# Attention and MoE on one core: inverse row sums by way of DRAM, their product on GpSimd, swapped queries by DMA, other buffer counts

## The chip, the cores and the metric

The kernel runs on one core of one Trainium2 chip. The metric is the device time of one execution in microseconds (us). A core has the engines TensorE (PE; its weight loads are shown apart as PEld), VectorE (DVE), ScalarE (ACT), GpSimd (POOL) and SyncE (SP), which issues nearly all DMAs here. Each engine runs its own instructions in order; semaphores order the engines among each other.

## The reference

Attention in which a query sees only the keys of its own hash bucket, then a gated MoE-like product over all tokens.

```python
# q, k, v: (4, 8, 768, 64), proj: (64, 6)
q_bits = np.einsum('bhsd,dk->bhsk', q, proj) > 0
k_bits = np.einsum('bhsd,dk->bhsk', k, proj) > 0
mask = q_bucket[:, :, :, None] == k_bucket[:, :, None, :]   # buckets: the 6 bits as a number
scores = np.where(mask, (1 / np.sqrt(D)) * q @ k.T, -1e9)
attn = np.exp(scores - scores.max(-1, keepdims=True))
attn = attn / (attn.sum(-1, keepdims=True) + 1e-9)
x = (attn @ v).transpose(0, 2, 1, 3).reshape(3072, 512)
gate = 1 / (1 + np.exp(-(x @ w_gate)))                      # w_gate, w_val: (512, 1536)
out = (gate * (x @ w_val)) @ w_out                          # w_out: (1536, 512)
```

## The kernel before

**Pairs and groups.** The 32 heads (4 batches of 8) are worked off in 16 pairs of heads (`pair`, L601). Each pair has 6 tiles of 128 queries, in two groups of three tiles (`group`, L696), so there are 32 groups.

**Preparing a pair.** `load` fetches k and q. The queries' tile `qr` has three columns of 64 for each row: head 0, head 1, head 0 again, so that `turn` (L626) can transpose both the pair (head 0, head 1), named q, and the swapped pair (head 1, head 0), named qs, from it. A turn is 12 small transposes on PE into a double PSUM bank (tag "two", three of them). `high` (L641) copies the result to SBUF in a rounded form (ACT or DVE), and `low` (L645, DVE) makes the rest, so that a product of high and low parts has nearly float32 precision. This gives kh/kl, qh/ql and qsh/qsl, two buffers of each. `hash_` multiplies with the projection on PE and `bits_q`, `bits_k` make +-masks on DVE (qb, kb). The pair's scores start only after all of `needs`: the low parts and the bits.

**Scores.** `scores(t, h)` is 8 matmuls (three products of high and low parts, and one of the bits, each in two row halves of the array), for 768 keys into a "two" bank. The swapped queries put head 1's queries into the rows of head 0's keys and the reverse, so both halves of the array work. `maximum` (L718, DVE) takes the row maximum and moves the scores to SBUF (tile `e`), `exponent` (L739, ACT) makes the exponentials in place and their row sums into a column of `su`.

**The rest of a group.** After its six exponentials: `guard` and `inverse` (DVE) turn the row sums into inverse sums, 6 columns of 128 rows. The product with v comes out transposed (head columns on partitions, queries along the row), so the inverse sums are needed along the row, the same on 64 partitions: `spread` (L754) does it by 6 matmuls of the broadcast column with the identity into a bank (tag "one"; each is two instructions, 12 in all), and `spread_copy` moves it to SBUF (`rb`). `turned(c)` (L768) transposes the probabilities of one chunk of 128 keys (12 transposes), `whole` copies them to SBUF (`ef`), and `values(c)` (L790) multiplies with v, four instructions a chunk, accumulated over six chunks in a "one" bank (`pv`). `summed` multiplies pv by rb on DVE into `xs`, and `store` sends it to the DRAM tensor xd.

**The MoE.** `moe_early` does a third of the hidden columns (J1 = 3 blocks of 128) of the first three batches, between the attention of later pairs; its units are spread over the scores' progress. `load_w` turns the weights from 64-bit floats into high and low parts on DVE, ACT and POOL, and keeps most of them in DRAM. After all stores of the attention, `switch` gives the attention's memory free, the kept weights are fetched, and `moe_late` does the rest. `load_x` and `gated` split x and the gated product into parts on ACT, POOL and DVE.

**Order.** Nothing of this is ordered by hand. Every step is added to a `Plan` (L58) with a key (its due place; t0 is 6 for each pair and 3 for each group), an engine or a choice of engines, an estimate of its ns, the steps it comes after, and the buffers that it takes and gives. `order` (L74) simulates the engines with these estimates and writes the steps in the order in which they start, so the estimates decide each engine's program order. `stock` counts the buffers. PE steps name the array's tiling: "rows" (two row halves: scores, transposes), "columns" (two column halves: spread, values) or all; the plan counts a change of it with 95 ns. 60 filler matmuls (`busy`, L270) stand at the lowest key.

Of the kernel before, what the change touches and what calls it, by code (L numbers as in the profile page):

```python
# [9 lines left out]
F32 = mybir.dt.float32  # L10
F32R = mybir.dt.float32r
# [8 lines left out]
P = 128  # L20
# [3 lines left out]
EPS = 1e-9  # L24
# [33 lines left out]
class Plan:  # L58
# [115 lines left out]
def lsh_attention_glu_kernel(ctx, tc, q, k, v, proj, w_gate, w_val, w_out, out):  # L174
    nc = tc.nc
    B, H, S, D = q.shape
# [3 lines left out]
    NC = S // P  # L180
    GT = 3
    NG = NC // GT
    GN = GT * P
    HP = H // 2
# [6 lines left out]
    f = lambda ap: ap.bitcast(F32)  # L191
# [4 lines left out]
    const = ctx.enter_context(tc.tile_pool(name="const", bufs=1))  # L196
    dram = ctx.enter_context(tc.tile_pool(name="dram", bufs=1, space=bass.MemoryType.DRAM))
    xd = [dram.tile([HP, P, S], F32, name=f"xd{b}") for b in range(B)]
    part = [dram.tile([NG, GT, P, DM], F32, name=f"part{b}") for b in range(B)]

    kept = {(n, j): dram.tile([P, 2, DM], F32, name=f"k{n}{j}") for n in "gvo" for j in range(J1, NJ)}
# [2 lines left out]
    ps = ctx.enter_context(tc.tile_pool(name="ps", bufs=2, space=PSUM))  # L204
    ident = const.tile([P, P], F32, name="ident")
# [37 lines left out]
    for n, signs, groups in (("q", (1.0, -1.0), ALL), ("k0", (-1.0, 1.0), ALL[::2]), ("k1", (-1.0, 1.0), ALL[1::2])):  # L243
        w = const.tile([P, P], F32, name=f"hw{n}", tag="hw")
        nc.vector.memset(w, 0.0)
        for g in groups:
            half = g % 2 if n == "q" else g // 2
            rows = slice(half * D, (half + 1) * D)
            for i, sign in enumerate(signs):
                at_ = g * HB + i * NB  # L250
                nc.vector.tensor_scalar_mul(w[rows, at_ : at_ + NB], praw[rows], sign)
        hi, lo = hw[n] = [const.tile([P, P], F32R, name=f"hw{n}{x}") for x in "hl"]
        nc.scalar.copy(hi, w)
        nc.vector.tensor_sub(lo, w, f(hi))
    mp = ctx.enter_context(tc.tile_pool(name="moe", bufs=1))
    xp = ctx.enter_context(tc.tile_pool(name="xp", bufs=1))
    w1 = ctx.enter_context(tc.tile_pool(name="w1", bufs=1))
# [2 lines left out]
    at = ph1.enter_context(tc.tile_pool(name="attn", bufs=2))  # L260
# [9 lines left out]
    def busy():  # L270
# [1 line left out]

    W_KEY, W_STEP = 12.0, 2.2
    stock = dict(
        one=1, two=3, moe=1, z=2, y=4, kr=2, qr=2, vr=2, h=2, e=10, st=3, su=3, rb=1, xs=2,
        ef=6, raw1=1, mid1=1, wk=1, xr=1, x=1, ob=3,
    )
    plan = Plan(stock)
    add = plan.add

    MM, MO, TH = 174, 231, 62
    FF = 644
# [3 lines left out]
    def dma(key, nbytes, emit, **kw):  # L286
        return add(key, "sp", 600, emit, tail=2000 + nbytes // 200, **kw)
# [300 lines left out]
    sp = lambda t: t.rearrange("p (j n) -> p j n", j=2)  # L588
# [3 lines left out]
    halves = [slice(0, D), slice(D, P)]  # L592


    def either(copied, n=1):
        return [
            ("act", 60 + 315 * n, lambda: copied(nc.scalar.copy)),
            ("dve", 70 + 400 * n, lambda: copied(nc.vector.tensor_copy)),
        ]

    def pair(i):  # L601
        b, hp = heads[i]
        u = f"{b}_{hp}"
        t0 = i * NC
        z = {}
        two = slice(2 * hp, 2 * hp + 2)

        def load(n):

            if n == "k":  # L610
                z[n] = at.tile([P, 2, GT, 2, D], F32, name=f"kr{u}", tag="kr", bufs=stock["kr"])
                from_ = k[b, two].rearrange("h (p c) d -> p h c d", c=NC)
                for h in range(2):
                    for j in range(2):
                        nc.sync.dma_start(z[n][:, h, :, j], from_[:, h, j * GT : (j + 1) * GT])
            else:
                z[n] = at.tile([P, NC, 3, D], F32, name=f"qr{u}", tag="qr", bufs=stock["qr"])
                from_ = q[b, two].rearrange("h (p c) d -> p h c d", c=NC)
                for m in range(3):
                    nc.sync.dma_start(z[n][:, :, m], from_[:, m % 2])  # L620

        def load_v():
            z["v"] = at.tile([P, 2, NC, D], F32, name=f"vr{u}", tag="vr", bufs=stock["vr"])
# [2 lines left out]
        def turn(n):  # L626

            z["t", n] = pt = ps2.tile([P, 2, 512], F32, name=f"t{n}{u}", tag="two")
            flat = z[n[0]].rearrange("p a b c d -> p (a b c d)" if n == "k" else "p a b d -> p (a b d)")
            step, first = (P, 0) if n == "k" else (3 * D, (n == "qs") * D)  # L630
            for m in range(NC):
                for r, rows in enumerate(halves):
                    nc.tensor.transpose(
                        pt[:, r, m * D : (m + 1) * D], flat[rows, m * step + first : m * step + first + P],
                        ident[rows, rows], tile_position=(r * D, 0),
                    )

# [6 lines left out]

        def low(n):  # L645
            nc.vector.tensor_sub(ordered(z[n + "l"]), turned_(n), f(ordered(z[n + "h"])))  # L646

        def hashed(acc, w, n, j):
            for m, (a, x) in enumerate(((1, "h"), (0, "l"), (0, "h"))):
# [21 lines left out]
            n: add(t0 - 10.72, "sp", 2400, lambda n=n: load(n), tail=4000, take=[n + "r"]) for n in "kq"  # L671
        }
        needs, last_turn = [], None
        for m, n in enumerate(("k", "q", "qs")):
            n_ = t0 - 6 + m
            last_turn = add(
                n_, "pe", 2 * NC * TH // 2 + 50, lambda n=n: turn(n), after=[here[n[0]], last_turn],
                take=["two"] + ["h"] * (m == 0), give=[n + "r"] if n == "k" else ["qr"] * (n == "qs"), tiles="rows",
            )
            a = add(n_, either(lambda copy, n=n: high(n, copy), 2), after=[last_turn])  # L680
            needs.append(add(n_, "dve", 880, lambda n=n: low(n), after=[a], give=["two"]))
        for m, n in enumerate("kq"):
            n_ = t0 - 2.8 + m * 0.6
            a = add(n_, "pe", 6 * MM, lambda n=n: hash_(n), after=[needs[m]], take=["two"])
            if n == "k":
                needs += [
                    add(n_, "dve", 590, lambda h=h: bits_k(h), after=[a], give=["two"] * h) for h in range(2)
                ]
            else:
                needs.append(add(n_, "dve", 990, bits_q, after=[a], give=["two"]))  # L690
        v_here = dma(t0 - 5, 393216, load_v, take=["vr"])

        for g in range(NG):
# [2 lines left out]
    def group(i, g, z, needs, v_here):  # L696
        b, hp = heads[i]
        u = f"{b}_{hp}_{g}"
        t0 = i * NC + g * GT
        gz = {}  # L700
# [36 lines left out]
            )  # L737

        def exponent(t, h):  # L739
            if t == 0 and h == 0:  # L740
                gz["su"] = at.tile([P, 2, GT], F32, name=f"su{u}", tag="su", bufs=stock["su"])
            e, st = gz["e", t, h], gz["st", t]
            nc.scalar.activation(  # L743
                e, e, AF.Exp, bias=st[:, 2, h : h + 1], scale=st[:, 1, h : h + 1],
                accum_out=gz["su"][:, h, t : t + 1],
            )

        def guard():
            nc.vector.tensor_scalar_add(gz["su"], gz["su"], EPS)

        def inverse():
            nc.vector.reciprocal(gz["su"], gz["su"])

        def spread():  # L754

            gz["rs"] = rs = ps.tile([P, 512], F32, name=f"rs{u}", tag="one")
            for t in range(GT):
                for h, rows in enumerate(halves):
                    nc.tensor.matmul(  # L759
                        rs[rows, t * P : (t + 1) * P], gz["su"][:, h, t : t + 1].broadcast_to([P, D]), ident,  # L760
                        start=True, stop=True, tile_position=(0, h * D),
                    )

        def spread_copy(copy):
            gz["rb"] = at.tile([P, GN], F32, name=f"rb{u}", tag="rb", bufs=stock["rb"])
            copy(gz["rb"], gz["rs"][:, :GN])

        def turned(c):  # L768

# [27 lines left out]
                    start=(c == 0), stop=(c == NC - 1), tile_position=(0, h * D),  # L797
                )

        def summed():  # L800
            gz["xs"] = at.tile([P, GN], F32, name=f"xs{u}", tag="xs", bufs=stock["xs"])
            nc.vector.tensor_mul(gz["xs"], gz["pv"][:, :GN], gz["rb"])

        def store():
            nc.sync.dma_start(xd[b][hp][:, g * GN : (g + 1) * GN], gz["xs"])
# [18 lines left out]
                    take=["su"] if t == 0 and h == 0 else [], give=["st"] * (h == 1),  # L824
                ))
        n = t0 - 0.78
        a = add(n, "dve", 90, guard, after=exps)
        inverse_ = add(n, "dve", 90, inverse, after=[a])
        chunks, last = {}, None
        for c in range(NC):  # L830
            n = t0 + LAG + c * 0.4
# [1 line left out]
                       give=["e"] * GT * 2 if c == NC - 1 else [], tiles="rows", kind="turn")  # L833
            chunks[c] = add(n, either(lambda copy, c=c: whole(c, copy), 2), after=[last], give=["two"])
        n = t0 + LAG + 3
        a = add(n, "pe", FF, spread, after=[inverse_], take=["one"], give=["su"], tiles="columns")
        spread_ = add(n, either(spread_copy), after=[a], take=["rb"], give=["one"])
        prev = None
        for c in range(NC):
            prev = add(  # L840
# [75 lines left out]
```

## Time and profile before

| | us |
|---|---|
| median of 3 runs (1119.0 to 1120.32) | 1119.46 |
| the profiled execution, own time | 1119.6 |
| its span, first to last instruction | 1117.8 |
| PE busy | 1095.1 |
| DVE busy | 564.8 |
| ACT busy | 505.1 |
| POOL busy | 231.6 |

In the profile, times are in us unless marked ns; L12 is line 12 of the kernel. A row of the groups by line gives line, engine, operation, output<-inputs, shapes and count, then total busy time and mean ns of one, then the engine's idle time just before them and what ended it. A row of the timeline gives start, length, engine, line and what was done, with neighbours of one kind merged. A row of the waits gives who waited for whom, the total, the number and the longest. PE's matmuls are pipelined, so lengths overlap: what a matmul costs in a row of others is the distance between starts. "q" behind an engine's name is its sequencer, which issues DMAs.

### The profile page before, as it was taken

To read this page: it belongs to the slowest core of one execution; us is meant where nothing else is said; L and a number is where in the kernel's file an instruction comes from. 1 tells how busy PE (TensorE), PEld (TensorE's weight loads), DVE (VectorE), ACT (ScalarE), POOL (GpSimd) and SP (SyncE) were. 2 spreads that over 40 slices of the span, in tenths; PEclk is the share of its full clock that TensorE was granted. 3 is DMA by queue.
4 is the path that set the end of the run, shared out by engine and by line. 5 is a ranking of instruction groups with operands and counts; after the bars stand their busy time and mean duration, and the time that the engine had idled before them with its cause. 6 is when DMAs were issued, how large, how long until landed. Compare 5 with 4: busy or idle time off the path is not lost.

```text
span 1117.8 us, 21374 instructions
## 1 busy us (share of the span) xinstructions
PE 1095.1 (98%) x8980; PEld 874.8 (78%) x8988; DVE 564.8 (51%) x1204; ACT 505.1 (45%) x898; POOL 231.6 (21%) x210
## 2 busy tenths in 40 slices
PE   9999999999999999999999999999999999999998
PEld 5666676677667677676667899999999999999997
DVE  7888878888879788887774101001020202020201
ACT  4766676667667676676665212212121212121211
POOL 0101224122324213312001112112121212121211
PEclk9999999999999999999999999999999999999999
DMA  8323343544544435531101860002020201010010
GB/s 189 89 61 97 106 135 99 157 148 151 169 139 140 140 120 162 179 126 54 49 15 46 320 242 28 31 1 85 1 85 1 69 17 59 26 51 34 7 51 28
DMA packets 110655, 103.61 MB, mean 93 GB/s; under 512 B 66784, under 2 KB 94432, under 8 KB 110560
## 3 DMA queue, kind: packets, MB, share of 16 engines
q1 hardware_dynamic: 110400, 102.26, 29.1%
q8 instruction: 70, 1.15, 0.4%
q14 instruction: 25, 0.20, 0.1%
q10 hardware_dynamic: 160, 0.00, 0.0%
HBM read 70.78 MB, written 31.46 MB: 91 GB/s over the span
## 4 chain that ended last, share of the span: by engine, by line
PE 84%; DVE 9%; POOL 2%; ACT 2%; issue 1%; POOLq 0%; DVEq 0%
PE pv L795 12%; PE sc L709 8%; PE zv_0l L424 7%; PE zv_1l L424 7%; PE zg_0l L424 7%; PE zg_1l L424 7%; PE yo_0l L457 7%; PE yo_1l L457 6%; PE tp L778 6%; DVE e L723 4%; PE zo L457 4%; PE zg L424 3%; PE zv L424 2%; PE sc L714 2%; PE rs L759 2%
## 5 line engine op out<-in xcount | busy, mean ns | idle before, releaser
L743 ACT ACTIVATE e<-e,st 128x768 f32<-128x768 f32 x192 | 196.7, 1026 | 77.6 <-DVE st L735 73.5
L723 DVE TENSOR_SCALAR_CACHE_REDUCE e<-sc 128x768 f32<-128x768 f32 x192 | 177.2, 951 | 32.7 <-PE sc L714 32.4
L795 PE MATMUL pv<-ef,vr 128*64 128x384 f32 x768 | 136.9, 494 | 0.3 <-issue 0.3
L440 DVE TENSOR_TENSOR gf_0l<-zv_0l,sig 128x384 f32<-128x384 f32 x39 | 21.7, 557 | 210.2 <-PE zv_0l L424 210.2
L440 DVE TENSOR_TENSOR gf_1l<-zv_1l,sig 128x384 f32<-128x384 f32 x39 | 21.8, 558 | 208.9 <-PE zv_1l L424 208.9
L778 PEld LDWEIGHTS tp<-ident,e 64*128 64x128 f32 x2304 | 81.7, 138 | 34.7 <-issue 18.3
L785 DVE COPY ef<-tp 128x768 f32<-128x768 f32 x99 | 91.6, 951 | 33.2 <-PE tp L778 32.8
L778 PE MATMUL tp<-ident,e 64*128 64x64 f32 x2304 | 95.9, 227 | 8.9 <-DVE ql L646 2.4
L795 PEld LDWEIGHTS pv<-ef,vr 128*64 128x64 f32 x768 | 49.8, 136 | 56.8 <-issue 44.6
L709 PE MATMUL sc<-kh,qsl 64*128 64x384 f32 x192 | 85.7, 447 | 2.2 <-DVE e L723 1.9
L424 PE MATMUL zg_0l<-xh_0l,wg 128*128 128x384 f32 x312 | 86.4, 337 | 0.0
L424 PE MATMUL zg_1l<-xh_1l,wg 128*128 128x384 f32 x312 | 86.4, 337 | 0.0
L709 PE MATMUL sc<-kh,ql 64*128 64x384 f32 x192 | 85.7, 447 | 0.3 <-issue 0.3
L424 PE MATMUL zv_1l<-xh_1l,wv 128*128 128x384 f32 x312 | 85.5, 334 | 0.0
L424 PE MATMUL zv_0l<-xh_0l,wv 128*128 128x384 f32 x312 | 85.5, 334 | 0.0
L785 ACT COPY ef<-tp 128x768 f32<-128x768 f32 x93 | 73.2, 796 | 25.5 <-PE tp L778 24.9
L445 POOL TENSOR_TENSOR gl<-gf_0l,gh 128x384 fp32r<-128x384 f32 x39 | 40.8, 1047 | 185.4 <-ACT gh L444 185.4
L445 POOL TENSOR_TENSOR gl<-gf_1l,gh 128x384 fp32r<-128x384 f32 x39 | 40.4, 1037 | 184.5 <-ACT gh L444 184.5
L457 PE MATMUL yo_0l<-wo,gh 128*128 128x512 f32 x234 | 73.5, 395 | 0.0
L457 PE MATMUL yo_1l<-wo,gh 128*128 128x512 f32 x234 | 73.5, 395 | 0.0
L576 ACT ACTIVATE sig<-zg_1l 128x384 f32<-128x384 f32 x39 | 19.2, 492 | 116.1 <-PE zg_1l L424 116.1
L576 ACT ACTIVATE sig<-zg_0l 128x384 f32<-128x384 f32 x39 | 19.2, 492 | 111.0 <-PE zg_0l L424 111.0
(165 smaller groups left out, 2572.2 us busy)
## 6 DMA issues: line engine op xcount, KB each, us to landing
qr<-in_q_dram SPq DMA_DIRECT2D x48, 192.0 KB, 4.0
kr<-in_k_dram SPq DMA_DIRECT2D x64, 96.0 KB, 2.6
vr<-in_v_dram SPq DMA_DIRECT2D x16, 384.0 KB, 3.7
rawg<-in_moe_w_gate_dram SPq DMA_DIRECT2D x12, 512.0 KB, 4.0
xd<-xs SPq DMA_DIRECT2D x32, 192.0 KB, 2.9
rawv<-in_moe_w_val_dram SPq DMA_DIRECT2D x12, 512.0 KB, 3.7
rawo<-in_moe_w_out_dram SPq DMA_DIRECT2D x12, 512.0 KB, 3.7
xr<-xd SPq DMA_DIRECT2D x6, 768.0 KB, 4.5
```

What stands on the lines that cost most here:

```text
L424: nc.tensor.matmul(z["acc"][:, :GN], a[:, wc], x[xx][:, c, :], start=(c == 0 and i == 0), stop=(c == KC - 1 and i == 2),)
L440: nc.vector.tensor_mul(z["gf"], z["acc"][:, :GN], sig[:, j])
L445: low = lambda eng: eng.tensor_sub(gl[:, j], z["gf"], f(gh[:, j]))
L457: nc.tensor.matmul(acc, a[:, slot, ts_], w, start=(first and i == 0), stop=(last and i == 2))
L576: lambda slot=slot, z=z: nc.scalar.activation(sig[:, slot], z["acc"][:, :GN], AF.Sigmoid),
L709: nc.tensor.matmul(sc[:, j, :GN], q_[rows, c], z["k" + x][rows, h * GN : (h + 1) * GN], start=(m == 0), stop=False, tile_position=(j * D, 0),)
L714: nc.tensor.matmul(sc[:, j, :GN], z["qb"][rows, c], z["kb"][rows, h], start=False, stop=True, tile_position=(j * D, 0),)
L723: nc.vector.tensor_scalar(sp(e), gz["sc", t, h][:, :, :GN], -SCALE, None, op0=ALU.mult, op1=ALU.min, accum_out=gz["st", t][:, 0, h : h + 1],)
L743: nc.scalar.activation(e, e, AF.Exp, bias=st[:, 2, h : h + 1], scale=st[:, 1, h : h + 1], accum_out=gz["su"][:, h, t : t + 1],)
L778: nc.tensor.transpose(tp[:, r, at_ : at_ + D], gz["e", t, h][rows, c * P : (c + 1) * P], ident[rows, rows], tile_position=(r * D, 0),)
L785: copy(gz["ef", c].rearrange("p (n r d) -> p r n d", r=2, d=D), gz["tp", c][:, :, :GN].rearrange("p r (n d) -> p r n d", d=D),)
L795: nc.tensor.matmul(gz["pv"][rows, :GN], z["v"][:, h, c], gz["ef", c][:, h * GN : (h + 1) * GN], start=(c == 0), stop=(c == NC - 1), tile_p ...
```

## The change

Four things change.

1. The inverse row sums no longer pass PE. They stand in one of three tiles `sums` of 128x32; after guard and reciprocal, a DVE transpose of 32x32 blocks puts them into `sv`, a DMA (`told`) writes `sv` to a DRAM tensor `rd`, and two DMAs (`spread`) read it back, broadcast to 64 partitions each, into `rb`.
2. `summed` only copies pv to xs (ACT or DVE); `divided` multiplies xs by rb in SBUF on POOL.
3. The queries are loaded without the third column and turned once. The swapped tiles qsh and qsl are copied from qh and ql by DMA, two DMAs each, the halves of the partitions exchanged. The scores of the pair wait for them.
4. Buffers: e 10 to 12, ef 6 to 4, rb 1 to 2, xs 2 to 3, sv 2 new.

```diff
+    rd = [dram.tile([32, P // 32, 32], F32, name=f"rd{i}") for i in range(B * HP * NG)]
...
+    sums = [const.tile([P, 32], F32, name=f"su{m}") for m in range(3)]
+    for m in range(3):
+        nc.gpsimd.memset(sums[m], 0.0)
...
-        one=1, two=3, moe=1, z=2, y=4, kr=2, qr=2, vr=2, h=2, e=10, st=3, su=3, rb=1, xs=2,
-        ef=6, raw1=1, mid1=1, wk=1, xr=1, x=1, ob=3,
+        one=1, two=3, moe=1, z=2, y=4, kr=2, qr=2, vr=2, h=2, e=12, st=3, su=3, sv=2, rb=2, xs=3,
+        ef=4, raw1=1, mid1=1, wk=1, xr=1, x=1, ob=3,
...
-                z[n] = at.tile([P, NC, 3, D], F32, name=f"qr{u}", tag="qr", bufs=stock["qr"])
+                z[n] = at.tile([P, NC, 2, D], F32, name=f"qr{u}", tag="qr", bufs=stock["qr"])
...
-                for m in range(3):
-                    nc.sync.dma_start(z[n][:, :, m], from_[:, m % 2])
+                for m in range(2):
+                    nc.sync.dma_start(z[n][:, :, m], from_[:, m])
...
+        def swapped(x):
+
+            z["qs" + x] = to = at.tile([P, S], F32R, name=f"qs{x}{u}", tag=f"qs{x}")
+            for r, rows in enumerate(halves):
+                nc.sync.dma_start(f(to)[rows], f(z["q" + x])[halves[1 - r]])
...
-        for m, n in enumerate(("k", "q", "qs")):
+        for m, n in enumerate("kq"):
...
+            if n == "q":
+                swaps = [add(n_, "sp", 1200, lambda x=x: swapped(x), after=[y], tail=4000) for x, y in (("h", a), ("l", needs[1]))]
...
+        needs += swaps
...
-        def guard():
-            nc.vector.tensor_scalar_add(gz["su"], gz["su"], EPS)
         def inverse():
-            nc.vector.reciprocal(gz["su"], gz["su"])
+            some = gz["su"][:, : 2 * GT]
+            nc.vector.tensor_scalar_add(some, some, EPS)
+            nc.vector.reciprocal(some, some)
+            gz["sv"] = at.tile([P, 32], F32, name=f"sv{u}", tag="sv", bufs=stock["sv"])
+            nc.vector.transpose(gz["sv"], gz["su"])
+
+        def told():
+
+            nc.sync.dma_start(rd[i * NG + g].rearrange("j b i -> b j i"), gz["sv"])
         def spread():
-            gz["rs"] = rs = ps.tile([P, 512], F32, name=f"rs{u}", tag="one")
-            for t in range(GT):
-                for h, rows in enumerate(halves):
-                    nc.tensor.matmul(
-                        rs[rows, t * P : (t + 1) * P], gz["su"][:, h, t : t + 1].broadcast_to([P, D]), ident,
-                        start=True, stop=True, tile_position=(0, h * D),
-                    )
-
-        def spread_copy(copy):
             gz["rb"] = at.tile([P, GN], F32, name=f"rb{u}", tag="rb", bufs=stock["rb"])
-            copy(gz["rb"], gz["rs"][:, :GN])
+            for h, rows in enumerate(halves):
+                row = rd[i * NG + g][h * GT : (h + 1) * GT].rearrange("j b i -> (j b i)").unsqueeze(0)
+                nc.sync.dma_start(gz["rb"][rows], row.broadcast_to([D, GN]))
...
-        def summed():
+        def summed(copy):
             gz["xs"] = at.tile([P, GN], F32, name=f"xs{u}", tag="xs", bufs=stock["xs"])
-            nc.vector.tensor_mul(gz["xs"], gz["pv"][:, :GN], gz["rb"])
+            copy(gz["xs"], gz["pv"][:, :GN])
+
+        def divided():
+            nc.gpsimd.tensor_mul(gz["xs"], gz["xs"], gz["rb"])
...
-        a = add(n, "dve", 90, guard, after=exps)
-        inverse_ = add(n, "dve", 90, inverse, after=[a])
+        a = add(n, "dve", 300, inverse, after=exps, take=["sv"], give=["su"])
+        a = add(n, "sp", 600, told, after=[a], tail=2500, give=["sv"])
+        spread_ = add(n, "sp", 1200, spread, after=[a], tail=3500, take=["rb"])
...
-        a = add(n, "pe", FF, spread, after=[inverse_], take=["one"], give=["su"], tiles="columns")
-        spread_ = add(n, either(spread_copy), after=[a], take=["rb"], give=["one"])
...
-        a = add(n - 4, "dve", 470, summed, after=[prev, spread_], take=["xs"], give=["one", "rb"])
+        a = add(n - 4, either(summed), after=[prev], take=["xs"], give=["one"])
+        a = add(n - 4, "pool", 1230, divided, after=[a, spread_], give=["rb"])
```

More of the change, by code (lines that the diff above doesn't have):

```diff
@@ L628, in turn @@
             z["t", n] = pt = ps2.tile([P, 2, 512], F32, name=f"t{n}{u}", tag="two")
-            flat = z[n[0]].rearrange("p a b c d -> p (a b c d)" if n == "k" else "p a b d -> p (a b d)")
-            step, first = (P, 0) if n == "k" else (3 * D, (n == "qs") * D)
+            flat = z[n].rearrange("p a b c d -> p (a b c d)" if n == "k" else "p a b d -> p (a b d)")
             for m in range(NC):
@@ L633, in turn @@
                     nc.tensor.transpose(
-                        pt[:, r, m * D : (m + 1) * D], flat[rows, m * step + first : m * step + first + P],
+                        pt[:, r, m * D : (m + 1) * D], flat[rows, m * P : (m + 1) * P],
                         ident[rows, rows], tile_position=(r * D, 0),
@@ L673, in pair @@
         needs, last_turn = [], None
-        for m, n in enumerate(("k", "q", "qs")):
+        for m, n in enumerate("kq"):
             n_ = t0 - 6 + m
             last_turn = add(
-                n_, "pe", 2 * NC * TH // 2 + 50, lambda n=n: turn(n), after=[here[n[0]], last_turn],
-                take=["two"] + ["h"] * (m == 0), give=[n + "r"] if n == "k" else ["qr"] * (n == "qs"), tiles="rows",
+                n_, "pe", 2 * NC * TH // 2 + 50, lambda n=n: turn(n), after=[here[n], last_turn],
+                take=["two"] + ["h"] * (m == 0), give=[n + "r"], tiles="rows",
             )
@@ L739, in exponent @@
         def exponent(t, h):
-            if t == 0 and h == 0:
-                gz["su"] = at.tile([P, 2, GT], F32, name=f"su{u}", tag="su", bufs=stock["su"])
+            gz["su"] = sums[(i * NG + g) % len(sums)]
             e, st = gz["e", t, h], gz["st", t]
@@ L744, in exponent @@
                 e, e, AF.Exp, bias=st[:, 2, h : h + 1], scale=st[:, 1, h : h + 1],
-                accum_out=gz["su"][:, h, t : t + 1],
+                accum_out=gz["su"][:, h * GT + t : h * GT + t + 1],
             )
-        def guard():
-            nc.vector.tensor_scalar_add(gz["su"], gz["su"], EPS)
         def inverse():
-            nc.vector.reciprocal(gz["su"], gz["su"])
-        def spread():
-            gz["rs"] = rs = ps.tile([P, 512], F32, name=f"rs{u}", tag="one")
-            for t in range(GT):
-                for h, rows in enumerate(halves):
-                    nc.tensor.matmul(
-                        rs[rows, t * P : (t + 1) * P], gz["su"][:, h, t : t + 1].broadcast_to([P, D]), ident,
-                        start=True, stop=True, tile_position=(0, h * D),
-                    )
-        def spread_copy(copy):
+            some = gz["su"][:, : 2 * GT]
[5 more added lines that the diff above has]
+            nc.sync.dma_start(rd[i * NG + g].rearrange("j b i -> b j i"), gz["sv"])
+        def spread():
             gz["rb"] = at.tile([P, GN], F32, name=f"rb{u}", tag="rb", bufs=stock["rb"])
-            copy(gz["rb"], gz["rs"][:, :GN])
+            for h, rows in enumerate(halves):
+                row = rd[i * NG + g][h * GT : (h + 1) * GT].rearrange("j b i -> (j b i)").unsqueeze(0)
+                nc.sync.dma_start(gz["rb"][rows], row.broadcast_to([D, GN]))
         def turned(c):
```

## The prediction

> **What bounds the kernel now.** First the page's totals, then the busy time of two windows, cut where the attention ends.
>
> ```profile
> span 1117.8 us, 21374 instructions
> PE 1095.1 (98%) x8980; PEld 874.8 (78%) x8988; DVE 564.8 (51%) x1204; ACT 505.1 (45%) x898; POOL 231.6 (21%) x210
> ```
>
> ```profile
> 0.00:620.00 620.00, 602.54 (x6410) 418.17 (x6419) 492.41 (x1094) 410.48 (x707) 134.51 (x118) 1.00 0.39 117
> 620.00:1118.00 498.00, 492.61 (x2572) 456.63 (x2570) 72.35 (x110) 94.59 (x192) 97.09 (x92) 1.00 0.18 63
> ```
>
> The columns of the second fence are length, then busy PE, PEld, DVE, ACT, POOL with counts, granted clock, DMA share, GB/s. Up to 620 us attention and the early part of the MoE run together; after it the MoE alone. The change touches the first stage only. There PE is busy for 602.5 of 620 us at clock 1.00, DVE for 79%, ACT for 66%. A busy PE might still be waiting inside its modelled ends, so I read how its instructions follow each other, and what ended its idle time.
>
> ```profile
> 380.78 0.35 PE L778 MATMUL tp<-ident,e 64*128 64x64 f32 x5
> 381.06 0.88 PE L759 MATMUL rs<-ident,su 128*64 128x128 f32 x12
> 381.86 0.59 PE L778 MATMUL tp<-ident,e 64*128 64x64 f32 x12
> ...
> 604.89 0.88 PE L759 MATMUL rs<-ident,su 128*64 128x128 f32 x12
> 605.70 1.33 PE L778 MATMUL tp<-ident,e 64*128 64x64 f32 x36
> ```
>
> ```profile
> PE tp L778 <- DVE ql L646: 2.4, 3, 1.2
> ```
>
> Each block starts before the one ahead has ended, and the longest total wait in the table of waits for PE is 2.4 us in three places. So **PE's own order of work is the bound of the first stage**: a block taken out of that order is worth the distance from its start to the next block's start. The chain of waits agrees but warns that DVE stands close behind:
>
> ```profile
> PE 84%; DVE 9%; POOL 2%; ACT 2%; issue 1%; POOLq 0%; DVEq 0%
> ```
>
> **The change part by part.** *The spread of the inverse sums (L759) leaves PE.* It ran once in each of the 32 groups. From the fence above, one block takes 381.86 - 381.06 = 0.80 us in mid-stage and 605.70 - 604.89 = 0.81 us at the end: 32 x 0.80 = 25.6 us.
>
> *The third turn of the queries (L633 on tqs) leaves PE,* once in each of 16 pairs.
>
> ```profile
> 394.63 0.58 PE L633 MATMUL tqs<-ident,qr 64*128 64x64 f32 x12
> ...
> 395.02 0.42 PE L709 MATMUL sc<-kh,qsl 64*128 64x384 f32 x1
> ```
>
> ```profile
> L633 PE MATMUL tqs<-ident,qr 64*128 64x64 f32 x192 | 9.1, 228 | 2.1 <-DVE ef L785 1.9
> L646 DVE TENSOR_TENSOR qsl<-tqs,qsh 128x768 fp32r<-128x768 f32 x16 | 15.2, 952 | 0.3 <-ACT qsh L643 0.3
> L802 DVE TENSOR_TENSOR xs<-pv,rb 128x384 f32<-128x384 f32 x32 | 17.8, 557 | 26.7 <-PE pv L795 21.9 <-ACT e L743 4.7
> L752 DVE RECIPROCAL su<-su 128x6 f32<-128x6 f32 x32 | 5.9, 185 | 0.1
> L445 POOL TENSOR_TENSOR gl<-gf,gh 128x384 fp32r<-128x384 f32 x16 | 17.0, 1066 | 120.4 <-ACT gh L444 120.4
> ```
>
> Start to start it is 0.39 us; busy with its tail it is 9.1/16 = 0.57 us. The group lies between 6.2 and 9.1 us; I take 0.45 each, nearer to the start-to-start row, 7.2 us.
>
> *DVE, ACT and POOL.* DVE loses qsl (15.2 us) and the product xs (17.8 us); the copy of pv to xs takes the place and the shape of the copy of rs to rb (either engine), so these two cancel. A 32x32-block transpose of 128x32 is not in the trace; the reciprocal's 185 ns on 6 columns and the product's 557 ns on 384 bound it, 6 to 18 us in all; I take 6, since 32 columns are nearer to 6. DVE thus falls by about 27 us, 5.5% of its 492.4 us in the stage, much like PE's 32.8 of 602.5 (5.4%). So DVE does not become the bound, and I charge nothing for it. POOL gains 32 products at 1.07 us, 34 us on an engine busy for 134.5 of 620; the idle POOL hides them.
>
> One thing speaks against giving POOL this product. DVE's xl subtraction, with two SBUF inputs and of the same shape as the product gf with one PSUM input, takes more than twice as long where POOL works at the same lines:
>
> ```profile
> L397 DVE TENSOR_TENSOR xl_1l<-xr_1l,xh_1l 128x384 fp32r<-128x384 f32 x8 | 9.4, 1215 | 1.2 <-ACT xh_1l L394 1.2
> L440 DVE TENSOR_TENSOR gf<-zv,sig 128x384 f32<-128x384 f32 x18 | 9.9, 551 | 8.5 <-PE zv L424 7.4 <-POOL gl L445 1.1
> ```
>
> At worst each new product costs DVE 1.215 - 0.551 = 0.66 us, 21 us in all, but nearly all of DVE's work in the stage reads PSUM (e, ef, kl, ql, qb). I take nothing, at most 2 us. The Trainium skill, "GPSIMD Engine Reference", section 1 (Specifications), says that the two engines contend for SBUF when the DVE instruction has two SBUF inputs or a 2-port mode; by that rule only the weight preparation and xl would suffer, which agrees with the two rows above.
>
> *Four buffers for turned chunks instead of six (ef).* The diff also cuts ef from 6 to 4. The fifth transpose of a group now waits for its first product with v, so a run of products longer than 4 chunks (16 matmuls) cannot stay whole. The chain in order of time has 12 pieces of 24 and 10 of 20, of which the first and the last are
>
> ```profile
> 34.77 4.02 PE pv L795 x24
> ...
> 100.95 3.40 PE pv L795 x20
> ...
> 486.03 3.38 PE pv L795 x20
> ...
> 573.83 4.02 PE pv L795 x24
> ```
>
> so 22 runs must break. What a break costs I read from a short run:
>
> ```profile
> 386.07 0.34 PE L714 MATMUL sc<-kb,qb 64*128 64x384 bf16 x2
> 386.34 4.09 PE L795 MATMUL pv<-ef,vr 128*64 128x384 f32 x24
> 390.36 0.59 PE L633 MATMUL tq<-ident,qr 64*128 64x64 f32 x12
> ...
> 595.68 0.87 PE L795 MATMUL pv<-ef,vr 128*64 128x384 f32 x4
> 596.48 0.45 PE L424 MATMUL zv<-xh,wv 128*128 128x384 f32 x1
> ```
>
> 24 take 4.02 us, 0.1675 each; a run of 4 takes 0.80 instead of 0.67, so 0.13 us for leaving. Entering takes 0.27 us after the pair of bias matmuls, against 0.17 us of stream: 0.10. With the second change of mode about 0.34 us a break: 22 x 0.34 = 7.5 us, between 0 (other blocks merge where rs stood) and 22 (twice in each group, 64 x 0.34). The Trainium skill, "TensorEngine Tiling (Array Packing)", Key Properties, says that changing the tiling mode drains the engine; it gives no price, and by it each break costs a drain on both sides, where the rows give the amounts above. Two more e buffers (12) let the scores run on while chunks are held longer; I set this against the longer hold, at nothing.
>
> *Swapped queries by DMA.* Each pair adds four SP issues and drops one, and a pair's first score now waits for the landing.
>
> ```profile
> qr<-in_q_dram SPq DMA_DIRECT2D x48, 192.0 KB, 4.0
> ...
> xd<-xs SPq DMA_DIRECT2D x32, 192.0 KB, 2.9
> ```
>
> ```profile
> 2.81 2.01 SPq L620 DMA_DIRECT2D qr<-in_q_dram  x3
> ```
>
> ```profile
> 393.65 0.95 DVE L646 TENSOR_TENSOR ql<-tq,qh 128x768 fp32r<-128x768 f32 x1
> ```
>
> ```profile
> 0.00:412.70 412.70, 99.50 (x792) 65.62 (x792) 1.00 0.45 131
> ```
>
> 792 = 11 x 72 matmuls of scores are issued before 412.7, so pair 11 starts there. Its ql is ready at 394.6, 18.1 us earlier. An issue takes 2.01/3 = 0.67 us, so four and a landing of 2.9 to 4.0 us take 5.6 to 6.7 us: hidden behind the previous pair's scores. If SP is held up for over 11 to 12 us, that cover is gone (first rival). Queued behind a waiting swap are loads of k, q, v and raw weights; q and k are loaded with two buffers, a pair ahead, and the weights are first needed in the MoE, so no one waits for a few microseconds there. In the first pair there is no pair ahead:
>
> ```profile
> 11.01 0.95 DVE L646 TENSOR_TENSOR ql<-tq,qh 128x768 fp32r<-128x768 f32 x1
> ```
>
> ```profile
> 15.52 0.44 PE L709 MATMUL sc<-kh,ql 64*128 64x384 f32 x1
> ```
>
> ql ends at 11.96 here, and would end sooner without qsh's cast; up to four issues and a landing later, 5.6 to 6.7 us, the first score stands at 15.5 to 18.7, and with loads queued ahead at 19.5, instead of 15.5. I take +2 us, bounds 0 and 4; turns of the next pair and fillers stand in that gap already.
>
> *Round trip of the inverse sums.* After the reciprocal: transpose 0.2, issue 0.3 and landing 2.9 at most (that was 192 KB, this is 16), on SP the spread waits for that landing, two issues 1.3 and landing 2.9: some 7.6 us, then POOL's product.
>
> ```profile
> 97.74 0.19 DVE L752 RECIPROCAL su<-su 128x6 f32<-128x6 f32 x1
> ```
>
> ```profile
> 104.38 0.56 DVE L802 TENSOR_TENSOR xs<-pv,rb 128x384 f32<-128x384 f32 x1
> ```
>
> ```profile
> 618.53 0.32 SPq L805 DMA_DIRECT2D xd<-xs  x1
> ```
>
> In this group, one of the tightest, pv is ready 6.4 us after the reciprocal, so the factor may come 1.2 us late there. Only POOL and one of three xs buffers wait for it: PE's bank goes free with the copy. Behind the waiting product stand POOL's steps of the weights, whose users come late, and the lower halves of x and of the gated products, which DVE can take too. At the end of the stage the last store (618.5) moves by a copy and a POOL product less the old product, about 1.1 us, and with it the weight fetches behind it; PE has resident weights to work on then, so I charge nothing.
>
> **Sum**, against the profiled execution (span 1117.8 us, its own time 1119.6, as is the median of the runs, 1119.46): -25.6 - 7.2 + 7.5 + 2 = -23.3, thus 1096 us.
>
> **The rivals.** *1, slower: SP's queue delays the swaps.* SP takes its DMAs in order, and the new ones wait on DVE, on a landing and on POOL (the stores).
>
> ```profile
> SPq L805 <- DVE xs L802: 83.2, 14, 18.3
> ```
>
> It has stood for up to 18.3 us before a store. A swap queued behind such a wait lands 18.3 + 5.6 us after ql, 5.8 us too late for the 18.1 us above. In half of the pairs that is 8 x 5.8 = 46 us, less the gain: 1142. It makes the kernel slower from 23.3/15 = 1.6 us a pair. Against it: such waits fall on one DMA in many, and the 144 added issues (64 swaps, 32 and 64 for the sums, less 16 loads) at 0.32 to 0.67 us fill only 46 to 96 of SP's 620 us.
>
> *2, no gain: four ef buffers make PE wait.* After a group's fourth transpose PE needs a product, then a transpose, a copy, and the last two products. A DVE pass over 128x768 is 0.95 us (ql above); where no score or MoE block stands between, 22 such waits cost 21 us: 1117. For it: the first four pairs have no MoE work. Against it: scores of the next group are mostly there.
>
> *3, more gain:* no break costs anything because transposes move next to scores, and the longer value of tqs counts: -25.6 - 9.1 = 1085; PSUM's freed double bank might add a few.
>
> **How the numbers follow.** Forecast 0.58, rival 1 0.14, rival 2 0.14, rival 3 0.14. The forecast's own bounds: -34.7 without breaks or start cost, -5.8 with 22 and 4 us: 1085 to 1114. Rival 3 extends it to 1082; 0.14 + part of rival 2 stay outside. A measurement of this kernel can tell about 0.2%, 2.2 us. Rival 2 lies around that bound: 0.05 faster, 0.06 same, 0.03 slower. Faster 0.77, same 0.06, slower 0.17.
>
> **What would show it.** Right: no L759 and no tqs, PE's blocks still overlapping in the first stage, that stage some 23 us shorter, the MoE stage as long as before; runs of pv of at most 16; PE's first score at 16 to 19 us. Wrong: PE waiting for a DMA into qsh or qsl beyond the first pair (rival 1); PE idle before pv or tp with ef as releaser (rival 2); DVE's share of the stage rising towards PE's.

## The result and the profile after

The changed kernel takes 1091.47 us (1089.71 to 1092.48 in 4 runs) against 1119.89 us before: 28.4 us less, a ratio of 0.9745 with a 95% interval of 0.9728 to 0.9762. The forecast was 1096 us, 23.3 us less, in a range of 1082 to 1114. So the time came out as forecast. The experiments below show that most of the terms in the sum, tried alone, did not.

First the page's totals of the changed kernel (span, then busy time of the engines), and the two windows that answer to those of before: the stage with attention now ends at 592 us, and the columns are those of the prediction.

```profile
span 1090.4 us, 20528 instructions
PE 1064.4 (98%) x8407; PEld 845.1 (78%) x8412; DVE 539.1 (49%) x1180; ACT 497.5 (46%) x891; POOL 262.5 (24%) x242
```

```profile
0.00:592.00 592.00, 571.63 (x5836) 388.16 (x5842) 466.77 (x1070) 404.11 (x701) 165.24 (x150) 1.00 0.50 150
592.00:1090.00 498.00, 492.79 (x2573) 456.94 (x2571) 72.34 (x110) 93.41 (x191) 97.28 (x92) 1.00 0.17 63
```

The second windows hold the same work on PE (2572 and 2573 matmuls in the trace) and are 498 us long in both, so all of the gain is in the first stage: 620 us became 592. Next, groups by line: the transposes and products of that stage, and the new instructions.

```profile
L805 PE MATMUL pv<-ef,vr 128*64 128x384 f32 x768 | 141.3, 498 | 2.1 <-DVE ef L795 1.7 <-ACT ef L795 0.3
L788 PE MATMUL tp<-ident,e 64*128 64x64 f32 x2304 | 94.7, 227 | 10.8 <-DVE e L736 6.2 <-ACT ef L795 1.6 <-DVE ef L795 1.1
L815 POOL TENSOR_TENSOR xs<-xs,rb 128x384 f32<-128x384 f32 x32 | 33.7, 1053 | 88.8 <-ACT xs L812 58.2 <-DVE xs L812 30.2
L812 ACT COPY xs<-pv 128x384 f32<-128x384 f32 x21 | 10.1, 480 | 27.0 <-PE pv L805 25.1 <-POOL gl L450 1.9
L765 DVE STREAM_TRANSPOSE sv<-su 128x32 f32<-128x32 f32 x32 | 6.8, 212 | 1.1
```

The transpose of the sums takes 212 ns (6 us were charged, 6.8 came), the product on POOL 1053 ns. POOL waits for the copies of pv (58.2 and 30.2 us), not for rb: the round trip through DRAM is hidden. The chain in order of time has 23 pieces of 16 products with v, of which these are the first and the last, and none longer:

```profile
47.98 2.73 PE pv L805 x16
...
562.50 2.73 PE pv L805 x16
```

The swaps are hidden too. Pair 11's last subtraction, its swaps on SP's queue, and the number of score matmuls that stand ahead of its first score (792 = 11 x 72):

```profile
365.72 0.95 DVE L650 TENSOR_TENSOR ql<-tq,qh 128x768 fp32r<-128x768 f32 x1
```

```profile
366.08 2.15 SPq L656 DMA_DIRECT2D qsh<-qh  x2
368.33 1.18 SPq L656 DMA_DIRECT2D qsl<-ql  x2
```

```profile
0.00:395.20 395.20, 99.28 (x792) 65.96 (x792) 1.00 0.54 159
```

The last issue ends at 369.5 us and the scores start at 395.2: 25.7 us are left for the landing. Only the first pair is late; its first score came at 15.52 us before.

```profile
19.19 0.44 PE L722 MATMUL sc<-kh,ql 64*128 64x384 f32 x1
```

### The profile page after: what moved, and what is told of

It reads as the page before. It is cut to its first block, busy times and chain, and to the rows that moved or that the text cites. A ratio compares the mean times of both kernels' runs of the same rounds, so it can differ in the third digit from the quotient of the medians.

```text
span 1090.4 us, 20528 instructions
## 1 busy us (share of the span) xinstructions
PE 1064.4 (98%) x8407; PEld 845.1 (78%) x8412; DVE 539.1 (49%) x1180; ACT 497.5 (46%) x891; POOL 262.5 (24%) x242
## 4 chain that ended last, share of the span: by engine, by line
PE 82%; DVE 8%; ACT 3%; POOL 3%; issue 2%; DMA 1%; SPq 1%; POOLq 0%; DVEq 0%
PE pv L805 11%; PE sc L722 8%; PE zv_0l L429 7%; PE zv_1l L429 7%; PE zg_0l L429 7%; PE zg_1l L429 7%; PE yo_0l L462 7%; PE yo_1l L462 7%; PE tp L788 6%; PE zg L429 3%; PE zo L462 3%; DVE e L736 3%; PE zv L429 3%; PE sc L727 2%; ACT e L755 1%
## 5 line engine op out<-in xcount | busy, mean ns | idle before, releaser
L805 PE MATMUL pv<-ef,vr 128*64 128x384 f32 x768 | 141.3, 498 | 2.1 <-DVE ef L795 1.7
L788 PEld LDWEIGHTS tp<-ident,e 64*128 64x128 f32 x2304 | 81.7, 139 | 41.2 <-issue 19.8
L795 DVE COPY ef<-tp 128x768 f32<-128x768 f32 x95 | 89.2, 952 | 38.5 <-PE tp L788 36.1
L795 ACT COPY ef<-tp 128x768 f32<-128x768 f32 x97 | 76.3, 796 | 33.4 <-PE tp L788 32.5
```

The costliest lines, as they stand in the source:

```text
L788: nc.tensor.transpose(tp[:, r, at_ : at_ + D], gz["e", t, h][rows, c * P : (c + 1) * P], ident[rows, rows], tile_position=(r * D, 0),)
L795: copy(gz["ef", c].rearrange("p (n r d) -> p r n d", r=2, d=D), gz["tp", c][:, :, :GN].rearrange("p r (n d) -> p r n d", d=D),)
L805: nc.tensor.matmul(gz["pv"][rows, :GN], z["v"][:, h, c], gz["ef", c][:, h * GN : (h + 1) * GN], start=(c == 0), stop=(c == NC - 1), tile_p ...
```

## The experiments

Three parts were taken apart: the way of the sums (with the product on POOL), the swap, and the buffers (12 e and 4 ef). All eight combinations were timed, each against the kernel before on the same chip. An x means that the part is in. The runs were made at different times and on more than one chip, and the kernel before took between 1119.77 and 1120.31 us in them, so a difference between two rows carries some 0.5 us of that as well. The two rows with the sums but without the swap have 1 rb and 2 xs, the other two with the sums 2 and 3.

| run | sums | swap | buffers | median us | before us | difference | ratio, 95% interval |
|---|---|---|---|---|---|---|---|
| sums_alone | x | | | 1117.94 | 1119.77 | -1.8 | 0.9983, 0.9973 to 0.9992 |
| swap_alone | | x | | 1104.13 | 1119.77 | -15.6 | 0.9865, 0.985 to 0.988 |
| buffers_alone | | | x | 1108.38 | 1119.77 | -11.4 | 0.9903, 0.9888 to 0.9917 |
| changed_old_buffers | x | x | | 1111.51 | 1119.77 | -8.3 | 0.9934, 0.9917 to 0.995 |
| swap_and_buffers | | x | x | 1100.34 | 1120.31 | -20.0 | 0.9823, 0.9808 to 0.9837 |
| sums_and_buffers | x | | x | 1111.25 | 1120.31 | -9.1 | 0.9926, 0.9909 to 0.9942 |
| changed kernel | x | x | x | 1091.47 | 1119.89 | -28.4 | 0.9745, 0.9728 to 0.9762 |

### The sums alone

The changed kernel with the third turn on PE again, and the old counts of e, ef, xs and rb. The core of the edit:

```diff
-        one=1, two=3, moe=1, z=2, y=4, kr=2, qr=2, vr=2, h=2, e=12, st=3, su=3, sv=2, rb=2, xs=3,
-        ef=4, raw1=1, mid1=1, wk=1, xr=1, x=1, ob=3,
+        one=1, two=3, moe=1, z=2, y=4, kr=2, qr=2, vr=2, h=2, e=10, st=3, su=3, sv=2, rb=1, xs=2,
+        ef=6, raw1=1, mid1=1, wk=1, xr=1, x=1, ob=3,
...
-        for m, n in enumerate("kq"):
+        for m, n in enumerate(("k", "q", "qs")):
...
-        needs += swaps
```

> The kernel before with only the sums' way changed: transpose, DRAM round trip, broadcast, copy and GpSimd product; third turn on PE, 10 e, 6 ef, 2 xs and 1 rb as before. PE-order theory: 32 blocks of 0.80 us leave PE and nothing else changes there: -25.6 us, 1094. Rival (DVE and ACT bound the stage with PE, so freed PE time turns into waiting): about half, 1107. Rival (the round trip holds something up, with a single rb): above 1107.

Measured: 1.8 us less. All 32 spread blocks are gone from PE, and nearly nothing came of it. The group of the transposes before and in this run, with PE's idle time ahead of them behind the second bar:

```profile
L778 PE MATMUL tp<-ident,e 64*128 64x64 f32 x2304 | 95.9, 227 | 8.9 <-DVE ql L646 2.4 <-DVE e L723 2.0 <-ACT e L743 1.4
```

```profile
L788 PE MATMUL tp<-ident,e 64*128 64x64 f32 x2304 | 96.5, 230 | 22.5 <-DVE e L736 10.1 <-DVE ef L795 4.3 <-ACT ef L795 3.5
```

The waits rose from 8.9 to 22.5 us; they end with a maximum (e) or a copy (ef), the two steps that give a PSUM double bank back. Counted from start to start, so that waits are in, the transposes take 18 us more than before, and the products with v, in 66 blocks instead of 58, take 6 us more: together they use up the 25.8 us of the spread blocks, all but some 2. The single rb is not what holds things up: in this run POOL waits only for the copies of pv, and ACT's copies of pv only for the products on PE. One such place in PE's timeline of this run:

```profile
297.64 0.58 PE L788 MATMUL tp<-ident,e 64*128 64x64 f32 x12 [0.77 <-DVE e L736]
299.84 0.59 PE L788 MATMUL tp<-ident,e 64*128 64x64 f32 x12 [1.61 <-DVE e L736]
300.80 1.54 PE L788 MATMUL tp<-ident,e 64*128 64x64 f32 x24 [0.37 <-ACT ef L795]
302.27 1.55 PE L805 MATMUL pv<-ef,vr 128*64 128x384 f32 x4
```

Four chunks take 4.63 us from 297.64 to 302.27; in the prediction's fence at 605.70, a row of 36 transposes (three chunks) is 1.33 us long. Two things are to be seen: waits of 1.61 and 0.37 us for a bank, and, from 300.8 on, slow work: 24 transposes in 1.54 us and four products in 1.55 (0.87 long in the prediction's short run). The windows around it give the reason; the third number from the right is the granted clock.

```profile
297.00:300.00 3.00, 0.75 (x16) 0.61 (x18) 2.93 (x10) 1.54 (x4) 1.26 (x1) 1.00 1.02 363
300.00:303.40 3.40, 3.03 (x40) 2.17 (x40) 2.87 (x5) 3.40 (x7) 0.00 (x0) 0.56 1.08 329
303.40:306.80 3.40, 3.40 (x48) 1.87 (x46) 3.37 (x5) 1.42 (x4) 1.88 (x2) 0.94 0.25 75
```

After 3 us in which PE was busy for 0.75, the clock is at about half for 3.4 us. This run has five such stretches (its mean clock over the span is 0.992), the kernel before has none. Each can cost PE half of 3.4 us, at most 8.5 us in all.

### The swap alone

The kernel before with `swapped` as in the change, the third turn and the third column of qr gone; sums and buffers as before.

```diff
+        def swapped(x):
+
+            z["qs" + x] = to = at.tile([P, S], F32R, name=f"qs{x}{u}", tag=f"qs{x}")
+            for r, rows in enumerate(halves):
+                nc.sync.dma_start(f(to)[rows], f(z["q" + x])[halves[1 - r]])
...
-        for m, n in enumerate(("k", "q", "qs")):
+        for m, n in enumerate("kq"):
```

> The kernel before with only the swapped queries by DMA; sums and buffers as before. PE-order theory: 16 turns leave PE (-7.2 to -8.6 us) and the first score comes 3.7 us later, as in the changed kernel: -4 to -5 us, 1115. Rival (SP's queue delays the swaps): slower than before, PE waiting at the starts of pairs.

Measured: 15.6 us less, three times what PE's blocks and the late start come to. From start to start the 16 turns account for 8.6 us of it; the scores take 5.9 us less than before and the transposes 2.8. Why they do, this run alone does not show. The rival with SP's queue falls: the table of PE's waits names no DMA.

### The buffers alone

```diff
-        one=1, two=3, moe=1, z=2, y=4, kr=2, qr=2, vr=2, h=2, e=10, st=3, su=3, rb=1, xs=2,
-        ef=6, raw1=1, mid1=1, wk=1, xr=1, x=1, ob=3,
+        one=1, two=3, moe=1, z=2, y=4, kr=2, qr=2, vr=2, h=2, e=12, st=3, su=3, rb=1, xs=2,
+        ef=4, raw1=1, mid1=1, wk=1, xr=1, x=1, ob=3,
```

> The kernel before with 12 e and 4 ef alone. My prediction's step: +7.5 us (22 breaks of pv runs at 0.34), 1127. By the profile of the changed kernel, with 14 more pv blocks than before and 3.4 us more in them: +3 to +5, 1123 to 1125. Rival (12 e let DVE and ACT run ahead, which is worth more than the breaks cost): below 1119.

Measured: 11.4 us less where the prediction charged 7.5 more. The rival was right about the time. The breaks hardly came: the products with v stand in 65 blocks instead of 58, and take 134.1 us from start to start, as before. What is gone is waiting ahead of the transposes, 1.6 us here against the 8.9 us of the kernel before in the row above; all of PE's idle time together falls from 18.9 to 9.0 us.

```profile
L778 PE MATMUL tp<-ident,e 64*128 64x64 f32 x2304 | 93.9, 226 | 1.6 <-DVE e L723 0.7 <-ACT e L743 0.6
```

### The changed kernel with the old buffers

```diff
-        one=1, two=3, moe=1, z=2, y=4, kr=2, qr=2, vr=2, h=2, e=12, st=3, su=3, sv=2, rb=2, xs=3,
-        ef=4, raw1=1, mid1=1, wk=1, xr=1, x=1, ob=3,
+        one=1, two=3, moe=1, z=2, y=4, kr=2, qr=2, vr=2, h=2, e=10, st=3, su=3, sv=2, rb=2, xs=3,
+        ef=6, raw1=1, mid1=1, wk=1, xr=1, x=1, ob=3,
```

> The changed kernel with 10 e and 6 ef as before the change. If the breaks cost what I charged: 7.5 us less, 1084; by the 3.4 us more in pv blocks: 1088. Rival (12 e and 4 ef are a gain where PE has less work): above 1092.

Measured: 1111.51 us, 20.0 us above the changed kernel. The rival was right again: sums and swap together bring 8.3 us without the buffers, less than the swap alone. All 34.4 us of spread blocks and third turns are gone from PE here as well, but the transposes take 19.1 us more from start to start than in the kernel before, and PE is idle for 32.6 us instead of 18.9.

### The swap, and the sums, each with the buffers

The swap_and_buffers run is swap_alone with 12 e and 4 ef. The sums_and_buffers run is the changed kernel with the third turn of sums_alone (2 xs and 1 rb).

> The kernel before with the swapped queries by DMA and 12 e, 4 ef; the sums still spread by PE. PE-order theory: the 32 spread blocks are on PE, so 25.6 us above the changed kernel, 1117. New theory (the loop of scores, maximum, exponentials and transposes through the PSUM double banks and e buffers sets the pace, PE's freed time is waited away): the parts add up without the sums, -15.6 - 11.4 us, 1093, within 3 us of the changed kernel.

> The changed kernel with the third turn on PE again (2 xs and 1 rb to make room); sums by DMA, 12 e, 4 ef. PE-order theory: the changed kernel plus 16 turns, 1091.5 + 8.6 - 3.7 (first score), 1096. New theory: the swap's part is missing, 1091.5 + 15.6, 1107, about as with the buffers alone (1108).

Measured: 1100.34 and 1111.25. Neither theory holds. The spread on PE costs 8.9 us here (1100.34 against 1091.47), a third of its 25.6 us of blocks, where PE-order said all and the new theory nothing. The third turn costs 19.8 us (1111.25 against 1091.47), more than twice its blocks. The smaller counts of xs and rb in the second run explain little of that: once, for 3.7 us, a spread waits for rb to come free, and POOL waits only for copies of pv.

### Four ef alone

```diff
-        ef=6, raw1=1, mid1=1, wk=1, xr=1, x=1, ob=3,
+        ef=4, raw1=1, mid1=1, wk=1, xr=1, x=1, ob=3,
```

> The kernel before with 4 ef and still 10 e. It parts the two buffer edits, of which both together gave -11.4 us. My prediction's step: breaks cost 3 to 7.5 us, 1123 to 1127, and the two further e then gave 14 to 19. New theory: e is held longer with 4 ef, so at 10 e the loop gets tighter: slower, 1122 to 1130. Rival (fewer ef help because products with v come sooner and switch less): 1108.

Measured: 1126.41 us, 6.1 us more (ratio 1.0055, 1.004 to 1.007). With 10 e this term of the sum came out by itself. The runs of products break into 80 blocks instead of 58, 22 more as forecast, and take 7.0 us more from start to start. Against the run with both buffer edits, each measured from the kernel before on its chip, the step from 10 to 12 e at 4 ef is worth 6.1 + 11.4 = 17.5 us. In that step the products go from 80 blocks back to 65 and lose the 7.0 us again, and the idle time ahead of the transposes goes from 11.1 to 1.6 us. What a shortage of e looks like is seen in the waits too: ACT stands before the exponentials until PE makes scores, four times in this run (first row), once in the kernel before (second row), never in the run with 12 e; a step of scores is what takes an e buffer in the plan.

```profile
ACT e L743 <- PE sc L714: 22.3, 4, 5.9
```

```profile
ACT e L743 <- PE sc L714: 3.2, 1, 3.2
```

### The swap, with the third turn still on PE

```diff
+        def again():
+            kept_ = z["t", "q"]
+            turn("q")
+            z["t", "q"] = kept_
...
             if n == "q":
+                add(n_, "pe", 2 * NC * TH // 2 + 50, again, after=[last_turn], take=["two"], give=["two"], tiles="rows")
```

> The kernel with the swap alone (1104.1), PE still making the third turn into a PSUM bank that nobody copies and that is given back at once. PE-order theory: 16 turns of 0.45 to 0.57 us come back: 1111 to 1113. New theory: what counted was DVE and ACT (the cast and the subtraction of qs, 28 us of their time) and the bank held through them: 1104 to 1107.

Measured: 1119.75 us (ratio 0.9995, 0.9986 to 1.0004): the whole gain of the swap is gone, though DVE and ACT are still spared 28 us. So the relief of DVE and ACT shows no gain while the turn is there, and a turn of half a microsecond that takes a double bank is worth about 1 us of the time. The plan's order is another one here too, so this is not the turn's length alone. The waits and the group of the turns in this run:

```profile
PE sc L723 <- DVE e L737: 7.8, 6, 3.8
PE tp L792 <- DVE e L737: 2.8, 9, 0.4
```

```profile
L632 PE MATMUL tq<-ident,qr 64*128 64x64 f32 x384 | 18.3, 230 | 3.0 <-DVE e L737 1.4 <-DVE ql L645 0.8 <-DVE kl L645 0.6
```

The turns take 8.9 us more from start to start than in swap_alone; scores now wait for a maximum, the step that gives their bank back, up to 3.8 us at a time (1.9 us in all before), and the clock drops to half three times. Which of the bank and the clock weighs more in the rest of the 15.6 us stays open.

### A shorter spread in the same order

To part PE's time from the plan's order, the estimates were left alone and only the emitted matmuls cut.

```diff
-            for t in range(GT):
-                for h, rows in enumerate(halves):
-                    nc.tensor.matmul(
-                        rs[rows, t * P : (t + 1) * P], gz["su"][:, h, t : t + 1].broadcast_to([P, D]), ident,
-                        start=True, stop=True, tile_position=(0, h * D),
-                    )
+            few = ident.bitcast(BF16)
+            for h, rows in enumerate(halves):
+                for a, b_ in ((0, 256), (256, GN)):
+                    nc.tensor.matmul(
+                        rs[rows, a:b_], few[:, :D], few[:, : b_ - a], start=True, stop=True, tile_position=(0, h * D),
+                    )
```

> The kernel before with every engine's order as before (the plan's estimates are untouched), but the 12 float32 matmuls of each spread replaced by 4 short bf16 ones on the identity; it leaves out the spread of the inverse sums, so the factor is not theirs. If PE's time bounds the stage within a given order (each block worth its distance from start to start): 32 blocks fall from 0.80 to about 0.3 us, -14 to -18 us, 1102 to 1106. If PE's freed time is waited away whatever the order: 1117 to 1120. With the first, it was the new order of the plan that ate the gain in the run with the sums alone.

Measured: 1112.58 us, 7.2 us less (ratio 0.9935, 0.992 to 0.995). The same place as in the prediction's fence, in this run:

```profile
375.70 1.33 PE L778 MATMUL tp<-ident,e 64*128 64x64 f32 x36
376.97 0.36 PE L760 MATMUL rs<-ident 128*64 128x256 bf16 x4
377.35 0.59 PE L778 MATMUL tp<-ident,e 64*128 64x64 f32 x12
```

The block is 0.38 us here and 0.46 in the mean over the 32 (every block still changes the tiling twice), so 32 x (0.80 - 0.46) = 10.9 us left PE and 7.2 came through, two thirds. Within a given order, then, PE's time is mostly on the path, but not wholly. The rest went into waiting: PE's idle time rises from 18.9 to 23.4 us. One kind of wait that grew is that of the transposes for a copy of turned chunks, which gives a double bank back (first row this run, second row before):

```profile
PE tp L778 <- DVE ef L785: 2.2, 6, 0.5
```

```profile
PE tp L778 <- DVE ef L785: 0.3, 1, 0.3
```

The copies of before at the place above show how a spread can stand in such a wait:

```profile
380.42 1.82 DVE L785 COPY ef<-tp 128x768 f32<-128x768 f32 x2 [0.33 <-PE tp L778]
```

Three chunks fill the three double banks, and the first is free when the first of these two copies of 0.95 us ends, at 381.4. The spread at 381.06 stood in that wait: without it the next transposes, which start at 381.86, could have come at about 381.4 by these rows, not at 381.06. In 17 of the 32 groups the spread stood between two transposes like this.

### One nanosecond in the plan

```diff
-    FF = 644
+    FF = 645
```

> The kernel before with one estimate of the plan raised by 1 ns (FF 644 to 645, the ns of a product with v or a spread): the same work, buffers and rules, other orders from the first tie on. If the plan's order is a draw, with which each edit above was mixed: off by 3 to 10 us, either way. If orders this near are all worth the same: 1119 to 1121.

> The changed kernel with the same estimate raised by 1 ns. If the order is a draw: off by 3 to 10 us from 1091.5, either way; else within 1 us.

Measured: 1122.0 us (ratio 1.0018, 1.0008 to 1.0027), 2.2 us more than the kernel before, and 1090.57 us, 0.9 us less than the changed kernel (ratios to the kernel before 0.9739 and 0.9745, with intervals that overlap). Of PE's rows in the trace some 3500 of 8980 stand elsewhere in the first, but fewer than 40 of 8407 in the second, so the second is hardly another order. One draw of another order thus moved the time by 2.2 us, less than feared. How widely such draws spread is not shown by one; the differences of 6 us and more above are larger than this one.

### The first pair turned by PE

The changed kernel, in which pair 0 alone loads its swapped queries (into an e buffer) and turns them on PE.

```diff
+                if i == 0:
+                    e = at.tile([P, S], F32, name="qsr", tag="e", bufs=stock["e"])
+                    z["qs"] = e.rearrange("p (c j d) -> p c j d", j=2, d=D)
+                    for m in range(2):
+                        nc.sync.dma_start(z["qs"][:, :, m], from_[:, 1 - m])
...
-        for m, n in enumerate("kq"):
+        for m, n in enumerate(("k", "q", "qs") if i == 0 else "kq"):
```

> The changed kernel, with the swapped queries of the first pair alone loaded swapped and turned on PE as before the change; the other 15 pairs by DMA. In the changed kernel the first score started 3.7 us later than before. If that start stands on the path: -2 to -4 us, 1088. If the order is a draw: anywhere within some 8 us of 1091.5, with the first score at 15 to 16 us all the same.

```profile
16.06 0.44 PE L729 MATMUL sc<-kh,ql 64*128 64x384 f32 x1
```

Measured: the first score comes 3.1 us sooner (16.06 against 19.19), the time is 1090.29 us, 1.2 less than the changed kernel and within what a nudge does (0.974, 0.9725 to 0.9755). The late start is not a term that can be told from nothing.

## Why the prediction came out, point by point

**The time was right; the sum holds for the whole change, but not for its parts.** The terms were -25.6, -7.2, +7.5 and +2; the parts gave, each alone, -1.8 (sums), -15.6 (swap with its start) and -11.4 (buffers). These three also add up to -28.8, near the -28.4 measured, but the combinations between do not add, so that is no law either. Counted from start to start on PE, the changed kernel against the kernel before does show the prediction's terms: -25.8 us of spread, -8.6 of third turns, +3.4 in the products with v, +0.9 in the transposes, -30.1 in all against the -28.4 measured. That holds because PE's idle time stays nearly the same, 18.9 and 21.8 us. With the same blocks gone and the old buffers it is 32.6 us, and most of the gain is lost. So the buffers, which the sum charged as a loss, are what lets the blocks count, and in that the forecast was lucky.

- *"A block taken out of that order is worth the distance from its start to the next block's start"*: this step failed. It holds where the next block is ready and waits only for PE. The rows that I quoted for it, spread between transposes, are a place where it was not: the next transpose waited for a double bank. Two thirds came through in the same order, 7% (1.8 of 25.6) where the plan re-ordered and no other resource was freed, a third (8.9) on top of swap and buffers. On top of one of the two alone, the sums' part even made the kernel slower: by 7.4 us with the swap (1104.13 to 1111.51) and by 2.9 us with the buffers (1108.38 to 1111.25).
- *What bounds the stage*: "PE's own order" was a part of it. The other part is the loop of scores, maximum, exponentials, transposes and copies through three double banks and the e buffers; for this the runs with 12 e and with the third turn speak, and the waits above. PE's busy time, 97% of the first stage and 99% of the second, gives no sign of it. PEld's share does differ, 67% (418 of 620 us) and 92% (457 of 498), but in the changed kernel's first stage, 28 us shorter, it is 66% (388 of 592), so no run shows that it is such a sign.
- *Four ef*: right by itself (22 breaks and 7.5 us forecast; 22 breaks and 6.1 us measured with 10 e), but not in the change: with 12 e the products merge again, and the changed kernel has 72 blocks, 14 more than before, which take 3.4 us more.
- *Twelve e "at nothing"*: the mis-sized term. With 4 ef it is worth 17.5 us. I had named the effect (scores run on while chunks are held) and set it against the longer hold without a number.
- *The third turn*: 7.2 us of blocks were charged; with its bank it is worth 6.4 to 19.8 us, by what else is there. That it holds one of three double banks through a cast and a subtraction was mentioned only in the third rival.
- *DVE*: "does not become the bound" held (467 of 592 us, 79% as before), and sparing DVE and ACT 28 us of work with the turn kept showed no gain. The two-input contention with POOL was bounded at 2 us; the weight steps with two SBUF inputs, 50.2 us of DVE before, take 51.6.
- *The swaps and the round trip*: hidden, as forecast. Rival 1 (SP's queue) did not come. The start is 3.7 us late (2 charged) and costs at most 1.2.
- *Rival 2* named PE waiting for buffers, but for ef and after the change. The waits were for the double banks and, by the runs with 10 and 12 e, for e, and they were there before it.

What the runs leave open: why the removal of the spread is worth -1.8 alone, +7.4 with the swap, +2.9 with the buffers and -8.9 last. The traces show the waits for banks and the clock's drops; the orders differ too much to say more, and the two nudged runs do not say how much of it is the luck of an order.

## What to carry to other kernels

A block removed from the busiest engine is worth its length only if its successor was ready: look at what the successor waits for (banks, copies) at the quoted place, not only at whether PE looks gapless. When work leaves an engine and buffers are re-cut in one change, put a price on each buffer count, the generous ones too. And test parts in combination: here sums and swap without the buffers were worth less than the swap alone.

## What the runs showed of the hardware that was not expected

The granted clock fell after waits much shorter than its own stretch of 3.4 us. In the run with the sums alone, PE was busy for 0.75 of 3.0 us, with a longest single wait of 1.61 us, and the clock fell to half for the next 3.4 us. Ahead of the last few us of a run, this came five times there, three times with the third turn kept, three with the changed kernel's old buffers, and once each in four other profiles, that of the changed kernel among them, but never in that of the kernel before. How little work brings it is not shown: the changed kernel's drop at 542.9 us followed 3.5 us in which PE was busy for 2.34, while 3.4 us with 0.97 busy passed without one in the run with the old buffers. Of four runs of the changed kernel, the two with a mean clock of 0.998 took 1092.19 and 1092.48 us, the two at 1.000 took 1090.74 and 1089.71. Half rate for 3.4 us accounts for at most 1.7 of these 2 us, and the waits that come with it may be the rest. The Trainium skill, "TensorE: Matmul & The Clock Gate", Part 1, gives a window of 3413 ns and half rate after an idle window; the length and the ratio agree with these rows, but the stretches given here ahead of a drop were not idle. A kernel whose PE begins to wait a little can thus pay up to 1.7 us more for each such place.
